# Attention and expert block on one core: the first 28 weight pieces begun in SBUF, their PSUM bank lent to attention

## The chip, the cores and the metric

The kernel runs on one core of one Trainium2 chip. The time is device microseconds (us) of that core, the median of several runs. The core has TensorE (PE: matrix products, written only to PSUM), VectorE (DVE), ScalarE (ACT), GpSimd (POOL) and SyncE (SP, which here only issues transfers). Each takes its instructions from its own queue, in the order in which they were put there. PSUM is a small memory of 8 banks; in this kernel one bank is one tile of 128 x 512 fp32. SBUF is the large on-chip memory.

## What is computed

```
q, k, v: 8 batches x 8 heads x 576 x 64, fp32
scores = q @ k^T / 8, masked by blocks of 64 (block_i >= block_j)
attn   = softmax(scores);  x = attn @ v, heads side by side: 4608 x 512
h = x @ w_in  (512 x 2048);  g = h * sigmoid(1.702 h)
out = g @ w_out (2048 x 512)
```

The weights arrive as 64-bit floats. The kernel reads them as pairs of 32-bit words and makes fp32 from them itself.

## The kernel before

**Attention** goes by 32 pairs of heads, n = 0 to 31, four pairs to a batch. For each pair, `prep` (L292) turns q and k with DVE transposes (L297), `score` (L305) writes q k^T into PSUM banks, `weigh` (L340) takes them out with DVE (L351) and applies exp on ACT (L358), `normalise` (L364) works out the reciprocal on DVE (L368, L371) and scales on POOL (L376). In the first eight pairs `flip` (L401) transposes the weights with TensorE through PSUM banks and ACT copies them out (L411, L424); later pairs use DVE and DMA (`turn`, L382). `av` (L429) multiplies by v, and ACT copies the two banks into `xr` (L450, L451).

**The experts** (`moe`, L509) go by 12 tiles of 384 tokens. A tile's hidden units go in 16 steps `fc`: 12 matmuls into the one bank `h` (tile `hp`), the gate on ACT and DVE (L562, L563), a rounding to a high part on ACT (L571) and the low part on POOL (L82, tile `gl`), and nine matmuls of the step before into `acc0` to `acc2`. Every product is made of three: high x high, low x high, high x low.

**Weight conversion.** The weights are 32 pieces of 128 x 512, in an order of w_in and w_out parts. Piece j goes through a chain: SP loads it (L202); `begin(j)` scales its high words on ACT into a tile `bits[j]` (L219); `merge(j)` shifts that tile in place on DVE (L223), joins the sign on DVE (L229, it reads the loaded words and `bits`), and joins the low word's bits on DVE (L234, words and `bits` in, tile `wm` out); `split_weights(j)` rounds to the high part on ACT (L243) and takes the low part on POOL (L82, tiles `wil` and `wol`). `convert` (L246) runs two steps per piece, first `merge(j)`, then `split_weights(j)`, the load of piece j+2 and `begin(j+1)`. The pace is `WEIGHTS_BY` (L36): 13 pieces by head 8, all 32 by head 14.5; the first token tile asks for its pieces too (L543).

Before the change `bits` is a PSUM tile in bank `w3`, one bank for all pieces. So `begin(j+1)` waits until `merge(j)` has read it out.

**Banks.** `bank()` (L89) hands attention its banks in turn. Until the experts begin (`turns["experts"]`, set by the first `split`, L485, which comes after the A V product of pair 3, asked for by pair 4) it turns over seven: `w0`, `w1`, `w2`, `acc0` to `acc2` and `h`. From then on it has `w0` to `w2`, and from pair 9 on `w3` too.

**Output buffers.** The tag `osb` in SBUF has three buffers of 128 x 512 fp32. They hold the rows of the output on their way out (L527), and, before the first output, part of the loaded words of pieces 28 to 31 (`wst`, L197). Pieces 0 to 27 (`2 * len(places)` is 28) are loaded in pairs into rooms that later hold weights (L192).

**Order of the work.** The order of TensorE's instructions is the program's (`mm`, `tr`, L98 to L102). On ACT, DVE, POOL and SP the instructions are put in order when the kernel is built, by their priority (program order, with some raised) and by when their inputs and buffers are expected to be free. The order inside a pair comes from the strings at L26 to L33, where digits are score chunks, `B`, `C` and `a` are flips, `V` the product with v and `L` the preparation of the next pair; `advance` (L592) fills in expert matmuls after each item.

Of the kernel before, what the change touches and what calls it, by code (L numbers as in the profile page):

```python
# [10 lines left out]
F32 = mybir.dt.float32  # L11
# [29 lines left out]
def attention_moe_kernel(  # L41
# [12 lines left out]
    P = 128  # L54
# [9 lines left out]
    HP = H // 2  # L64
# [3 lines left out]
    d2 = ctx.enter_context(tc.tile_pool(name="d2", bufs=2))  # L68
    ps = ctx.enter_context(tc.tile_pool(name="ps", bufs=1, space=PSUM))

    def f(ap):
        return ap.bitcast(F32)
# [13 lines left out]
    turns = {"n": 0, "bank": 0, "experts": False}  # L86
    conv = {"step": 0, "loaded": 0}

    def bank():  # L89
        tags = ["w0", "w1", "w2"]  # L90
        if not turns["experts"]:
            tags += ["acc0", "acc1", "acc2", "h"]
        elif turns["n"] > 2 * HP:
            tags.append("w3")
        turns["bank"] += 1
        return ps.tile([P, 512], F32, tag=tags[turns["bank"] % len(tags)], name="bank")
# [17 lines left out]
    WC = 512  # L114
# [69 lines left out]
    places = [f"{n}{p}{g}" for n, g in (("wo", 3), ("wo", 2), ("wi", 3), ("wi", 2), ("wo", 3), ("wi", 3), ("wo", 3)) for p in "hl"]  # L184
# [28 lines left out]
    bits, whole = {}, {}  # L213

    def begin(j):

        bits[j] = ps.tile([P, 512], F32, tag="w3", name="wm")
        for w, c in parts[j]:
            nc.scalar.activation(out=bits[j][:, c], in_=f(w[..., 1]), func=AF.Copy, scale=2.0**-112)  # L219

# [25 lines left out]
    def convert(upto):  # L246

        while conv["step"] < int(2 * upto):
            j, odd = divmod(conv["step"], 2)
            if odd:  # L250
                split_weights(j)
                if j + 1 < len(pieces):
                    load_weights(j + 3)
                    begin(j + 1)
            else:
                if j == 0:
                    begin(0)
                merge(j)
            conv["step"] += 1
# [45 lines left out]
    def score(n, banks):  # L305
# [6 lines left out]
        for chunks in banks:  # L312

            part = []
            for lo, hi in ((0, 512),) if width(chunks[0]) <= 512 else ((0, 256), (256, S)):
                ss = [bank() for _ in range(2)]
                c = 0
                for i in chunks:
                    a, z = qrange(i)
                    w = min(hi, width(i)) - lo  # L320
                    for hd in range(2):
                        r = slice(hd * D, hd * D + D)

                        mm(
                            out=ss[hd][:, c : c + w], lhsT=qk[n][r, 0, a : a + P],
                            rhs=qk[n][r, 1, lo : lo + w], start=True, stop=True,
                        )
                        part.append((i, hd, lo, lo + w, ss[hd][0 : z - a, c : c + w]))
                    c += w
            todo.append(sorted(part, key=lambda x: (chunks[::-1].index(x[0]), x[2])))  # L330
# [70 lines left out]
    def flip(n, chunks):  # L401

        for i in chunks:
            todo = [(j, hd) for j in range(i) for hd in range(2)]
            for x in range(0, len(todo), 4):
                part = todo[x : x + 4]
                bk = bank()
                for y, (j, hd) in enumerate(part):
                    tr(out=bk[:, y * P : (y + 1) * P], in_=es[i][:, hd, j * P : (j + 1) * P], identity=ident)
                s0 = SLOT[i] + part[0][0]  # L410
                nc.scalar.copy(  # L411
                    out=pw[:, :, s0 : s0 + len(part) // 2].rearrange("p b s h c -> p (s h) b c"),
                    in_=bk[:, 0 : len(part) * P].rearrange("p (x b c) -> p x b c", b=4, c=32),
                )

        bk = bank()
        todo = [(i, hd) for i in chunks for hd in range(2)]
        for y, (i, hd) in enumerate(todo):
            tr(out=bk[0:BLK, y * P : (y + 1) * P], in_=es[i][:, hd, i * P : width(i)], identity=ident)
        src = bk[0:BLK, 0 : len(todo) * P].rearrange("p (x b c) -> p x b c", b=4, c=32)  # L420
        for part in ([0], [1]) if 0 in chunks else (chunks,):
            i, x, a = part[0], 2 * chunks.index(part[0]), 2 if part[0] else 0
            s0 = 9 + max(i, 1)
            nc.scalar.copy(  # L424
                out=pw[0:BLK, a : a + 2, s0 : s0 + len(part)].rearrange("p b s h c -> p (s h) b c"),
                in_=src[:, x : x + 2 * len(part), a : a + 2],
            )
# [237 lines left out]
```

## Time and profile before

| what | value |
|---|---|
| median of 3 runs | 1122.7 us (1121.84 to 1124.51) |
| the profiled execution, its own time | 1120.49 us |
| its span in the trace | 1118.6 us |
| mean granted TensorE clock | 0.992 |
| TensorE matmul busy, weight loads | 1076.4 us (96%), 908.7 us (81%) |
| DVE, ACT, POOL busy | 583.0, 498.6, 406.7 us |

The trace is one execution. Its rows give the start in us from the span's start, the duration in us, the engine, the line in the kernel, the operation, the tile written and those read, the number of instructions merged in the row, and in brackets the idle time before it with what ended that. "PE bank L102 <- ACT turned L411" reads: TensorE's write of a bank by the helper at L102 waited for ACT's write of `turned` at L411. Where a helper issues all the work (L99, L102, L82), the tile names tell which work it is. Times of single instructions are in us in a timeline and in ns where the text says so.

### The profile page before, as it was taken

The page shows a single profiled execution, that of the slowest core. Times are in us where ns is not written, and L with a number is a line of the kernel's source. Part 1 is how long each engine was busy: PE and PEld are TensorE (multiplying, and loading weights), DVE is VectorE, ACT ScalarE, POOL GpSimd, SP SyncE. Part 2 cuts the span into 40 slices and gives each one's busy share as a digit, 9 for nine tenths or more (in the row PEclk, how much of TensorE's full clock was granted, in tenths as well). Part 3 has the DMA queues.
Part 4 walks back from the last instruction along what each step waited for, and adds up shares of the span by engine and source line. Part 5 has one row for each costly group of instructions (what it writes and reads, how often), then busy time and mean ns, then how long its engine had stood idle before and what let it go on. Part 6 is the DMA issues. An engine that isn't in the chain of part 4 may idle for free. (4 is left out here: it accounts for less than half of the span.)

```text
span 1118.6 us, 19977 instructions
## 1 busy us (share of the span) xinstructions
PE 1076.4 (96%) x6960; PEld 908.7 (81%) x6960; DVE 583.0 (52%) x1856; ACT 498.6 (45%) x1321; POOL 406.7 (36%) x509
## 2 busy tenths in 40 slices
PE   5969998999999999999999999999999999999998
PEld 3757776788888888888888888888888888899997
DVE  6776885545545555654555655645545654211210
ACT  5866776434534433534443543444434444322322
POOL 4665664333333332333333333333333233122222
PEclk9979999999999999999999999999999999999999
DMA  8734532332444432343443333344342332200000
GB/s 171 205 89 153 150 73 62 84 79 57 105 86 86 103 80 64 64 98 78 98 101 74 75 93 65 70 108 85 81 107 63 71 85 58 54 29 1 29 1 29
DMA packets 219365, 91.25 MB, mean 82 GB/s; under 512 B 197760, under 2 KB 197760, under 8 KB 219264
## 3 DMA queue, kind: packets, MB, share of 16 engines
q1 hardware_dynamic: 214528, 89.38, 34.0%
q10 hardware_dynamic: 4736, 0.59, 0.3%
q8 instruction: 55, 0.90, 0.3%
q14 instruction: 46, 0.38, 0.1%
HBM read 45.09 MB, written 9.44 MB: 49 GB/s over the span
## 5 line engine op out<-in xcount | busy, mean ns | idle before, releaser
L82 POOL TENSOR_TENSOR gl<-g,gh 128x384 fp32r<-128x384 f32 x192 | 194.7, 1014 | 551.5 <-ACT gh L571 449.1
L99 PE MATMUL hp<-xh,wih 128*128 128x384 f32 x768 | 264.7, 345 | 7.9 <-DVE g L563 6.9
L563 DVE SCALAR_TENSOR_TENSOR g<-g,hp 128x384 f32<-128x384 f32 x192 | 105.9, 552 | 319.1 <-ACT g L562 317.8
L99 PE MATMUL hp<-xh,wil 128*128 128x384 f32 x768 | 258.4, 336 | 0.1
L562 ACT ACTIVATE g<-hp 128x384 f32<-128x384 f32 x192 | 94.1, 490 | 359.8 <-PE hp L99 354.8
L99 PE MATMUL hp<-xl,wih 128*128 128x384 f32 x768 | 253.9, 338 | 0.4 <-DVE xl L82 0.4
L99 PE MATMUL acc<-woh,gh 128*128 128x512 f32 x576 | 233.9, 406 | 0.0
L99 PE MATMUL acc<-wol,gh 128*128 128x512 f32 x576 | 226.9, 394 | 0.0
L99 PEld LDWEIGHTS hp<-xh,wih 128*128 128x128 f32 x768 | 144.2, 188 | 34.1 <-DVE g L563 23.1
L99 PE MATMUL acc<-woh,gl 128*128 128x512 f32 x576 | 167.9, 393 | 0.3 <-POOL gl L82 0.3
L571 ACT CAST gh<-g 128x384 fp32r<-128x384 f32 x192 | 98.4, 513 | 156.5 <-DVE g L563 156.4
L99 PEld LDWEIGHTS hp<-xh,wil 128*128 128x128 f32 x768 | 144.3, 188 | 6.5 <-POOL wil L82 0.7
L358 ACT ACTIVATE e<-e,mx 64x64 f32<-64x64 f32 (+4 forms) x240 | 132.3, 552 | 37.6 <-DVE mx L351 37.6
L376 POOL TENSOR_TENSOR e<-e,sm 64x64 f32<-64x64 f32 (+1 forms) x192 | 113.6, 612 | 95.0 <-DVE sm L371 46.5
L99 PEld LDWEIGHTS hp<-xl,wih 128*128 128x128 f32 x768 | 143.6, 188 | 1.3 <-DVE xl L82 1.3
L99 PE MATMUL bank<-qk 64*128 64x320 f32 (+4 forms) x768 | 122.5, 428 | 14.5 <-DVE qk L297 11.1
L99 PEld LDWEIGHTS acc<-woh,gh 128*128 128x128 f32 x576 | 107.9, 187 | 34.2 <-issue 10.5
L99 PEld LDWEIGHTS acc<-woh,gl 128*128 128x128 f32 x576 | 107.8, 188 | 25.9 <-POOL gl L82 1.2
L99 PEld LDWEIGHTS acc<-wol,gh 128*128 128x128 f32 x576 | 108.3, 188 | 16.7 <-POOL wol L82 0.3
L351 DVE CUSTOM_DVE_ANT_0 e<-bank,mask 64x64 f32<-64x64 f32 (+4 forms) x240 | 89.7, 417 | 56.9 <-PE bank L99 52.8
L385 DVE STREAM_TRANSPOSE turned<-e 128x384 f32<-128x384 f32 (+1 forms) x192 | 92.3, 499 | 48.8 <-POOL e L376 48.3
L99 PEld LDWEIGHTS bank<-qk 64*128 64x128 f32 x768 | 69.6, 193 | 54.2 <-issue 25.4
(50 smaller groups left out, 956.0 us busy)
## 6 DMA issues: line engine op xcount, KB each, us to landing
turned<-turned SPq DMA_DIRECT2D x192, 80.0 KB, 2.1
turned<-turned SPq DMA_DIRECT2D x96, 112.0 KB, 2.2
raw<-in_q_dram SPq DMA_DIRECT2D x128, 72.0 KB, 2.4
out_dram<-osb SPq DMA_DIRECT2D x36, 256.0 KB, 2.2
raw<-in_k_dram SPq DMA_DIRECT2D x120, 72.0 KB, 2.6
turned<-turned SPq DMA_DIRECT2D x96, 88.0 KB, 2.1
words<-in_moe_w_in_dram SPq DMA_DIRECT2D x16, 512.0 KB, 6.3
vp<-in_v_dram SPq DMA_DIRECT2D x60, 128.0 KB, 2.4
```

Source lines behind the costliest of these rows:

```text
L82: eng.tensor_tensor(out=out, in0=in0, in1=in1, op=ALU.subtract)
L99: return tc.keep_in_program_order(nc.tensor.matmul(**kw))
L351: nc.vector.tensor_tensor_reduce(out=e[0:m, hd, lo:hi], in0=s, in1=mk, op0=ALU.add, op1=ALU.min, scale=-0.125, scalar=3e38 if lo == 0 else ...
L358: nc.scalar.activation(out=e[0:m, hd], in_=e[0:m, hd], func=AF.Exp, scale=-1.0, bias=mx[0:m, i, hd : hd + 1], accum_out=sm[0:m, i, hd : hd ...
L376: nc.gpsimd.tensor_tensor(out=x, in0=x, in1=sc.to_broadcast([m, width(i)]), op=ALU.mult)
L385: nc.vector.transpose(out=tw[:, :, SLOT[i] : SLOT[i] + i, hd].rearrange("p b j c -> p j b c"), in_=e[:, hd, 0 : i * P],)
L562: nc.scalar.activation(out=g, in_=hp[:, 0:tt], func=AF.Tanh, scale=1.702)
L563: nc.vector.scalar_tensor_tensor(out=g, in0=g, scalar=1.0, in1=hp[:, 0:tt], op0=ALU.add, op1=ALU.mult)
L571: nc.scalar.copy(out=gh, in_=g)
```

## The change

`bits[j]` of pieces 0 to 27 becomes an SBUF tile under the tag `osb`, three buffers in turn. Pieces 28 to 31 stay in `w3`. `bank()` includes `w3` as long as fewer than 56 conversion steps (two for each of the 28 pieces) have been made, and, as before, from pair 9 on. So attention turns over eight banks before the experts begin, four from then until the last four pieces, three from there to pair 8, and four after. No instruction is added or taken away.

```
         tags = ["w0", "w1", "w2"]
         if not turns["experts"]:
             tags += ["acc0", "acc1", "acc2", "h"]
-        elif turns["n"] > 2 * HP:
+        if turns["n"] > 2 * HP or conv["step"] < 4 * len(places):
             tags.append("w3")
...
     def begin(j):

-        bits[j] = ps.tile([P, 512], F32, tag="w3", name="wm")
+
+        if j < 2 * len(places):
+            bits[j] = d2.tile([P, WC], F32, tag="osb", name="wb", bufs=3)
+        else:
+            bits[j] = ps.tile([P, WC], F32, tag="w3", name="wb")
         for w, c in parts[j]:
             nc.scalar.activation(out=bits[j][:, c], in_=f(w[..., 1]), func=AF.Copy, scale=2.0**-112)
```

## The prediction

> **What bounds the kernel now.** I read the page first, then the table of windows over the time in which weights are converted, then TensorE's timeline there, then the rows of the conversion's tile `wm`, then DVE, ACT and GpSimd around the stalls.
>
> The page, span and first engine line:
>
> ```profile
> span 1118.6 us, 19977 instructions
> PE 1076.4 (96%) x6960; PEld 908.7 (81%) x6960; DVE 583.0 (52%) x1856; ACT 498.6 (45%) x1321; POOL 406.7 (36%) x509
> ```
>
> TensorE bounds the kernel, and its work isn't touched. What an edit can win is TensorE's idle time, and this edit acts only while pieces 0 to 27 are converted, from the start to about 166 us. Five windows from 28 to 168 us, header and sum (after the time: each engine's busy us):
>
> ```profile
> core 0: us, PE busy (x) PEld busy (x) DVE busy (x) ACT busy (x) POOL busy (x), PEclk, DMA share, GB/s
> sum 140.00, PE 124.80 PEld 98.44 DVE 106.91 ACT 100.16 POOL 88.93; mean PE 24.96 PEld 19.69 DVE 21.38 ACT 20.03 POOL 17.79
> ```
>
> TensorE is idle for 140 - 124.8 = 15.2 us there, DVE is busy for 76% and GpSimd for 64%. TensorE's timeline shows which idle times end with a bank coming free (score or transpose into `bank`) and which with data:
>
> ```profile
> 47.49 1.53 PE L99 MATMUL bank<-qk 64*128 64x320 f32 x6 [0.90 <-DVE mx L351]
> ...
> 58.69 0.76 PE L99 MATMUL bank<-qk 64*128 64x192 f32 x8 [2.52 <-DVE qk L297]
> ...
> 63.16 2.37 PE L102 MATMUL bank<-ident,turned 128*128 128x128 f32 x10 [3.12 <-ACT xr L450]
> 66.33 3.88 PE L99 MATMUL bank<-qk 64*128 64x320 f32 x8 [0.80 <-ACT turned L424]
> ...
> 100.58 0.63 PE L102 MATMUL bank<-ident,turned 128*64 128x128 f32 x4 [1.42 <-ACT turned L411]
> ...
> 129.40 0.63 PE L102 MATMUL bank<-ident,turned 128*64 128x128 f32 x4 [1.60 <-ACT turned L411]
> ...
> 157.62 0.63 PE L102 MATMUL bank<-ident,turned 128*64 128x128 f32 x4 [0.46 <-ACT turned L411]
> ```
>
> L411, L424, L450 and L351 each empty a bank, and none writes what the waiting score or transpose reads: these waits are for a bank. Only the 2.52 us for `qk` is data.
>
> **Part 1: one bank more for attention.** After the experts begin, flips 2 and 3 take four banks out of three: the fourth (the x4 group) waits until the first is copied out. With four banks it takes the bank of a score that DVE had read earlier. So 1.42 + 1.60 + 0.46 = 3.48 us go. What comes next, the matmuls of `hp`, has its inputs long before. In the first four pairs the bank is used again after eight turns and not seven: 0.90 us go at 47.49. At 63.16 the flip of pair 3 takes B1 to B4: B1 was free, B2 is seven turns after the first bank of pair 3's A V product, and so waits for `xr`. With eight, B2 finds a free bank and B3 waits instead: 4 of the 10 transposes, 4/10 x 2.37 = 0.95 us, move into the wait. At 66.33 the first head's bank no longer waits for L424, the second's 4 of 8 matmuls are 1.9 us later: 0.80 us go. Sum of part 1: -6.1 us. It isn't more if ACT keeps its order, since these two ACT copies come late:
>
> ```profile
> 62.44 0.58 ACT L451 COPY xr<-bank 128x512 f32<-128x512 f32 x1
> ...
> 65.87 0.41 ACT L424 COPY turned<-bank 64x128 f32<-64x128 f32 x2
> ```
>
> **Part 2: the conversion's own instructions.** Rows of `wm` (min/median/max in ns), the copy to SBUF at L243, and who waited:
>
> ```profile
> L223 DVE TENSOR_SCALAR wm<-wm x32: 658/699/700, 18.1 to 180.3; 128x512 uint32<-128x512 uint32 x32
> L219 ACT ACTIVATE wm<-words x28: 612/633/662, 13.2 to 159.3; 128x512 f32<-128x512 f32 x28
> L229 DVE SCALAR_TENSOR_TENSOR wm<-words,wm x28: 660/693/697, 18.8 to 160.7; 128x512 uint32<-128x512 uint32 x28
> L234 DVE SCALAR_TENSOR_TENSOR wm<-words,wm x28: 639/682/689, 19.8 to 161.7; 128x512 uint32<-128x512 uint32 x28
> L243 ACT CAST wih<-wm x16: 605/620/631, 20.5 to 162.4; 128x512 fp32r<-128x512 f32 x16
> ...
>   DVE wm L223: 15.9, 18
> ```
>
> L219 into SBUF: the nearest row is L243, of the same size and written to SBUF, 620 ns beside 633, so 28 x 0.013 = 0.4 us less on ACT to, say, as much more; ACT isn't the last to finish at these stalls by that much, and I take nothing. L229 and L234 with both inputs in SBUF: the nearest rows are an expert subtraction with both inputs in SBUF, and a scaling wholly in SBUF for L223:
>
> ```profile
> L82 DVE TENSOR_TENSOR xl<-xr,xh x48: 543/557/1284, 76.2 to 1043.8; 128x384 fp32r<-128x384 f32 x48
> ```
>
> ```profile
> L378 DVE TENSOR_SCALAR e<-e,sm x48: 511/517/521, 212.5 to 951.2; 128x576 f32<-128x576 f32 x48
> ```
>
> 557 ns for 384 elements is no faster per element than 693 for 512, so L229 and L234 cost the same when nothing is in the way. L378 does 576 elements in 517 ns; L223 on 512 should fall from 0.70 to between 0.46 (in proportion) and 0.52: I take 0.48, 28 x 0.22 = -6.2 us of DVE. If uint32 shifts don't have that speed, it is 0.
>
> **Part 3: DVE and GpSimd in each other's way.** That maximum of 1284 ns is the price of part 2. DVE, then GpSimd, at two places:
>
> ```profile
> 56.38 0.91 DVE L368 TENSOR_SCALAR sm<-sm 128x2 f32<-128x2 f32 x1
> ...
> 73.00 0.15 DVE L368 TENSOR_SCALAR sm<-sm 128x2 f32<-128x2 f32 x1
> ...
> 76.24 2.14 DVE L82 TENSOR_TENSOR xl<-xr,xh 128x384 fp32r<-128x384 f32 x2 [0.47 <-PE bank L99]
> ```
>
> ```profile
> 55.45 1.81 POOL L376 TENSOR_TENSOR turned<-turned,sm 128x448 f32<-128x448 f32 x2
> ...
> 76.72 1.25 POOL L376 TENSOR_TENSOR turned<-turned,sm 128x448 f32<-128x448 f32 x1
> ```
>
> The same two-element L368 takes 0.15 us alone and 0.91 when it starts inside GpSimd's work: it ends at 57.29, 0.03 after GpSimd's 57.26. The two subtractions took 2.14 us where two medians are 1.11, and GpSimd's own instruction beside them 1.25, where the pair above gives 0.91. So a DVE instruction wholly in SBUF (L368's kind) or with two SBUF inputs (L82's kind) and a GpSimd instruction go one after the other. Today no conversion row shows it: L223 to L234 have minimum and maximum within 50 ns, though GpSimd is busy for 64% of the time. After the change all three, 84 instructions, are of these kinds.
>
> The Trainium skill, SBUF — State Buffer, section "Who interferes with whom", says this as a rule: an instruction of DVE with two SBUF inputs, or in a mode that uses both its ports, and one of GpSimd exclude each other, the later one blocking until the first is done. It speaks against this change, and the rows above agree with it. By its words a blocked instruction waits for the whole rest; the sum would then have half a GpSimd instruction (0.43 us) a time, 84 x 0.635 x 0.43 = 22.9, and the forecast below would be 1.6 us later.
>
> My own price: the 104 GpSimd instructions of the window average 88.93/104 = 0.86 us; half is 0.43, and 0.12 of the blocked instruction lies within the wait (0.15 - 0.03). So 0.635 x 0.31 = 0.20 us each. From below, all of L368 between 28 and 168 us (busy us, mean ns):
>
> ```profile
> L368 DVE TENSOR_SCALAR sm<-sm 128x2 f32<-128x2 f32 x24 | 7.4, 308 | 4.1 <-ACT turned L358 3.6
> ...
> L368 DVE TENSOR_SCALAR sm<-sm 64x2 f32<-64x2 f32 x6 | 1.8, 306 | 0.4 <-ACT turned L358 0.3
> ```
>
> 9.2 - 30 x 0.15 = 4.7 us of waiting, 0.16 each; from above, the two subtractions, (2.14 - 1.11)/2 = 0.52. I take 0.20, near the lower: 84 x 0.20 = 16.8 us more, less 6.2, so DVE has 10.6 us more in a window with 33.1 us idle.
>
> How much of that reaches TensorE? Behind a blocked L223, L229 or L234 in DVE's queue stand the gate L563, score reads L351 and the transposes L297. Who waited for L368 in the window:
>
> ```profile
>   POOL turned L376: 0.8, 1
>   PEld bank L99: 0.4, 1
> ```
>
> With the 0.76 us at 56.38, which stood ahead of the L297 that ended TensorE's 2.52 us idle time, TensorE felt 0.4 + 0.76 = 1.2 of 4.7 us, a quarter. The gate's slack agrees with less than the whole:
>
> ```profile
> 91.12 0.55 DVE L563 SCALAR_TENSOR_TENSOR g<-g,hp 128x384 f32<-128x384 f32 x1 [0.84 <-ACT g L562]
> ```
>
> ```profile
> 92.83 0.33 PE L99 MATMUL hp<-xh,wih 128*128 128x384 f32 x1
> ```
>
> Here the bank `h` is free at 91.67 and wanted at 92.83: one block of up to 1.16 us is hidden, two in a row aren't. So part 3 costs TensorE 10.6/4 = +2.7 us, between 0 (all in slack) and 10.6.
>
> **Part 4: the buffers `osb` and SP's queue.** Pieces 28 and 29 are loaded into `osb` too. Before, three loads found three buffers; now `bits[27]` holds one, and the load of piece 29 must wait until `merge(28)` is over. In SP's queue it already stands for long, and behind it are the loads of later heads:
>
> ```profile
> 146.71 18.04 SPq L202 DMA_DIRECT2D wst<-in_moe_w_out_dram  x4
> ```
>
> ```profile
> 169.38 0.75 DVE L234 SCALAR_TENSOR_TENSOR wm<-wst,wm 128x256 uint32<-128x256 uint32 x2
> ```
>
> ```profile
> 175.15 1.29 POOL L82 TENSOR_TENSOR wol<-wm,woh 128x512 fp32r<-128x512 f32 x1 [1.52 <-ACT woh L243]
> ```
>
> ```profile
> 180.91 0.39 PE L99 MATMUL acc<-woh,gh 128*128 128x512 f32 x1
> ```
>
> `merge(28)` ends at 170.1, and SP is held till then and not till 164.8. Piece 29 is whole at 176.4 and used at 180.9: a load that begins 5.3 us later meets 4.5 us of cover: between 0 and 0.8 us, and I take 0; without the cover it is 5.3.
>
> **Sum.** -6.1 + 2.7 + 0 = -3.4 us. On the profiled execution, 1120.5 us in all (1118.6 span), that gives 1117.1; the median of the runs is 2.2 us higher than this execution, so 1122.7 - 3.4 = 1119.3. The parts' bounds give 1116.6 (nothing of part 3 is felt) to 1127.2 (all of it).
>
> **Rivals.** First, **DVE fills up** (slower). If every conversion instruction meets GpSimd as the two subtractions did, 0.52 us each, DVE gets 84 x 0.52 - 6.2 = 37.5 us more and has 33.1. The 4.4 us over reach TensorE whole, of the rest a quarter, 8.3: 12.7 - 6.1 = +6.6, 1129.3. Place: 56 to 168 us, at `hp` behind L563 and at scores behind L297. It cancels the gain from 24.4 us net, that is (24.4 + 6.2)/84 = 0.36 us each. For it: once both queues are full they take turns, a whole instruction each. Against: 0.16 on L368. The Trainium skill's section named above is the same mechanism as a rule, and it doesn't say how often the two meet.
>
> Second, **the knot at 56 to 74 us comes loose** (faster). One `w3` forces L219 behind the last merge; DVE waited 15.9 us for it, 18 times. With three buffers L219 can be put earlier, ACT then doesn't hold L451 behind conversions, and the 3.12 us go whole, 2.2 more. With less idle time the clock may hold. Windows of 4 us, and the same groups at full clock:
>
> ```profile
> 64.00:68.00 4.00, 3.20 (x13) 2.20 (x12) 3.24 (x14) 3.22 (x13) 1.28 (x2) 0.50 0.87 225
> ```
>
> ```profile
> 34.52 1.98 PE L99 MATMUL bank<-qk 64*128 64x320 f32 x8
> 36.42 1.31 PE L102 MATMUL bank<-ident,turned 128*128 128x128 f32 x10
> ...
> 70.14 2.39 PE L102 MATMUL bank<-ident,turned 128*128 128x128 f32 x10
> ```
>
> At a granted 0.50 the scores took 3.88 and not 1.98, the transposes 2.37 and 2.39 and not 1.31: 4.0 us. Together -6.2 more: 1113.1. Against it: the 2.52 us for `qk` isn't a bank's, stands ahead of the clock's fall, and hangs on the DVE queue that the change loads more.
>
> Third, **given back**: TensorE meets the next late thing instead (scaled weights from GpSimd, a `qk`), or the order on ACT comes out the same; the gain of part 1 halves to 3 and part 3 takes it: 1122.7.
>
> **How the numbers follow.** Forecast 0.42, DVE fills up 0.26, knot 0.14, given back 0.18. The runs lie 2.7 us apart, so 0.2% (2.2 us) is about what can be told from no change. Faster: 0.36 of the forecast's 0.42, and the knot: 0.50. Same: 0.05 and 0.15 of the third: 0.20. Slower: the first rival, 0.01 and 0.03: 0.30. The range goes from the knot with part 3 unfelt, 1110.4, to the full DVE, 1129.3, rounded to 1110.5 and 1130. The forecast's own is 1116.6 to 1121.9, with from nothing to half of part 3's 10.6 felt.
>
> **What the profile after would show.** Right: no idle time at the x4 transposes after 84 us; L223 at about 480 ns at its least; L223, L229 and L234 spread up to 1.5 us, DVE busy up by some 10 us between 28 and 168. Wrong: L223 to L234 as tight as now (no exclusion, then -6 or better); mean blocks over 0.36 us; TensorE's idle time between 28 and 168 above 15.2 us; or no half clock around 60 to 74.

## The result and the profile after

| kernel | median, us | runs, us | ratio to before, 95% interval |
|---|---|---|---|
| before | 1122.27 | 1120.21 to 1124.51 | |
| changed | 1158.36 | 1155.55 to 1161.04 | 1.0321 (1.0288 to 1.0354) |

The change makes the kernel slower by 3.2%, some 36 us, where 3.4 us less had been forecast; the time lies outside the range. The profiled execution of the changed kernel took 1155.55 us (span 1153.8), 35.1 us more than that of before. Of the runs of the experiments, one of the kernel with bits in SBUF and the order of before took 5908 us; it is left out of that kernel's median and ratio.

In the code of the changed kernel the lines are 4 further down: L223 is `begin` on ACT, L227, L233 and L238 are the three steps of `merge` on DVE, L247 is the rounding on ACT, L355 the score read, L415 and L428 the copies of the flips, L454 and L455 those of A V.

The page of the changed kernel, its span and the engines' busy times:

```profile
span 1153.8 us, 19969 instructions
PE 1094.3 (95%) x6960; PEld 920.8 (80%) x6960; DVE 603.8 (52%) x1856; ACT 500.1 (43%) x1321; POOL 414.6 (36%) x509
```

TensorE does the same instructions in the same order in both kernels. Its busy time grew by 17.9 us (1076.4 to 1094.3) and its idle time, the span less the busy time, by 17.3 (42.2 to 59.5). DVE has 20.8 us more in as many instructions, GpSimd 7.9, ACT 1.5.

The table of windows over the time of the conversion, of before (first) and after; the columns are PE, PEld, DVE, ACT and POOL busy us, then TensorE's granted clock, the share of the DMA engines and GB/s:

```profile
56.00:84.00 28.00, 19.03 (x127) 14.56 (x126) 22.30 (x53) 17.17 (x48) 17.02 (x19) 0.76 0.35 89
...
140.00:168.00 28.00, 27.38 (x192) 21.47 (x191) 22.79 (x60) 20.59 (x54) 19.30 (x21) 1.00 0.31 72
```

```profile
56.00:84.00 28.00, 20.05 (x150) 14.51 (x150) 25.98 (x57) 18.05 (x48) 17.41 (x18) 0.67 0.36 89
...
140.00:168.00 28.00, 26.48 (x150) 21.11 (x152) 19.19 (x50) 14.72 (x40) 14.51 (x18) 0.76 0.25 60
sum 140.00, PE 113.64 PEld 89.01 DVE 105.75 ACT 85.41 POOL 78.80; mean PE 22.73 PEld 17.80 DVE 21.15 ACT 17.08 POOL 15.76
```

TensorE is now idle for 140 - 113.6 = 26.4 us there, and not 15.2. And the clock falls, after 140 us from 1.00 to 0.76 (0.50 in the first 12 us of that window): that is where the longer busy time comes from, the same matmuls at a lower clock. Between 140 and 168 us TensorE is nearly as busy as before, with 150 instructions and not 192. DVE's and ACT's rows look lighter, but each instruction of the program comes later, so a window holds less of it. At the end of the conversion the delay is whole: the last `begin` of a piece in SBUF starts at 195.4 us, in the kernel before at 159.3.

The rows of the tile `wb` in the changed kernel (min/median/max in ns), and below them who waited:

```profile
L227 DVE TENSOR_SCALAR wb<-wb x32: 405/424/1493, 17.1 to 214.6; 128x512 uint32<-128x512 uint32 x32
L223 ACT ACTIVATE wb<-words x28: 644/672/698, 13.0 to 195.4; 128x512 f32<-128x512 f32 x28
L233 DVE SCALAR_TENSOR_TENSOR wb<-words,wb x28: 675/691/1646, 18.2 to 196.5; 128x512 uint32<-128x512 uint32 x28
L238 DVE SCALAR_TENSOR_TENSOR wm<-words,wb x28: 675/1433/2709, 19.7 to 197.3; 128x512 uint32<-128x512 uint32 x28
...
  ACT woh L247: 19.8, 11
  ACT wih L247: 18.5, 15
```

The shift fell to 405 ns at its least, from 699 in the middle. But each of the three DVE steps, which all had a minimum and a maximum within 50 ns, now reaches 1.5 to 2.7 us, and half of the last ones take over 1.4 us. A piece of the changed kernel's timeline shows what they meet; DVE, then GpSimd:

```profile
130.54 0.42 DVE L227 TENSOR_SCALAR wb<-wb 128x512 uint32<-128x512 uint32 x1
130.88 1.78 DVE L238 SCALAR_TENSOR_TENSOR wm<-words,wb 128x512 uint32<-128x512 uint32 x1
132.59 0.68 DVE L233 SCALAR_TENSOR_TENSOR wb<-words,wb 128x512 uint32<-128x512 uint32 x1
...
133.53 1.75 DVE L238 SCALAR_TENSOR_TENSOR wm<-words,wb 128x512 uint32<-128x512 uint32 x1
```

```profile
130.75 1.37 POOL L82 TENSOR_TENSOR wol<-wm,woh 128x512 fp32r<-128x512 f32 x1 [1.61 <-ACT woh L247]
133.39 1.34 POOL L82 TENSOR_TENSOR wil<-wm,wih 128x512 fp32r<-128x512 f32 x1 [1.28 <-ACT wih L247]
```

L238 of one piece starts 0.13 to 0.14 us after GpSimd has begun the low part of the piece before, and ends 0.54 after GpSimd's end (132.66 against 132.12): it has waited out nearly the whole subtraction. Its own result lets ACT round, and ACT lets GpSimd begin the next subtraction, again just ahead of the next L238. So the chain keeps step with itself, 2.6 us a piece. What stands on ACT behind such a rounding is late; ACT, then TensorE, of the changed kernel:

```profile
137.93 0.62 ACT L247 CAST wih<-wm 128x512 fp32r<-128x512 f32 x1 [1.05 <-DVE wm L238]
...
138.87 0.25 ACT L428 COPY turned<-bank 64x128 f32<-64x128 f32 x1
139.02 0.66 ACT L223 ACTIVATE wb<-words 128x512 f32<-128x512 f32 x1
139.58 0.25 ACT L428 COPY turned<-bank 64x128 f32<-64x128 f32 x1
```

```profile
111.26 0.88 PE L102 MATMUL bank<-ident,turned 128*128 128x128 f32 x6 [2.29 <-DVE mx L355]
...
139.88 1.43 PE L99 MATMUL bank<-qk 64*128 64x320 f32 x2 [5.44 <-ACT turned L428]
...
142.69 0.52 PE L99 MATMUL hp<-xh,wih 128*128 128x384 f32 x1
```

The score at 139.88 waits 5.44 us for a bank that the second L428 empties, and the expert matmul after it takes 0.52 us where the same kind took 0.33 at full clock (92.83, above). The idle time at the x4 transposes is gone, as forecast, as long as attention has four banks (behind the last four pieces, where it has three, one of 1.25 us stands at 221.28 us), but waits of another kind and of up to 5.4 us stand elsewhere. The row at 111.26 is such a flip of 14 transposes: its last six wait for the bank of a score that DVE now reads late.

The build lays the order of ACT, DVE, POOL and SP anew for a changed program. Against before, 205 of ACT's 1008 places hold another instruction, 236 of DVE's 1472, 75 of POOL's 506 and 10 of SP's. So two things changed at once: what the instructions do, and their order.

### The profile page after: what moved, and what is told of

Its sections match the earlier page's. It is cut to its first block, busy times and chain, and to the rows that moved or that the text cites. A ratio compares the mean times of both kernels' runs of the same rounds, so it can differ in the third digit from the quotient of the medians.

```text
span 1153.8 us, 19969 instructions
## 1 busy us (share of the span) xinstructions
PE 1094.3 (95%) x6960; PEld 920.8 (80%) x6960; DVE 603.8 (52%) x1856; ACT 500.1 (43%) x1321; POOL 414.6 (36%) x509
## 5 line engine op out<-in xcount | busy, mean ns | idle before, releaser
L99 PE MATMUL bank<-qk 64*128 64x320 f32 (+4 forms) x768 | 127.2, 435 | 27.8 <-DVE qk L301 9.9
L355 DVE CUSTOM_DVE_ANT_0 e<-bank,mask 64x64 f32<-64x64 f32 (+4 forms) x240 | 89.6, 416 | 56.8 <-PE bank L99 52.7
```

The source lines that it names most:

```text
L99: return tc.keep_in_program_order(nc.tensor.matmul(**kw))
L355: nc.vector.tensor_tensor_reduce(out=e[0:m, hd, lo:hi], in0=s, in1=mk, op0=ALU.add, op1=ALU.min, scale=-0.125, scalar=3e38 if lo == 0 else ...
```

## The experiments

The theory: DVE's steps wholly in SBUF, or with two SBUF inputs, and GpSimd's instructions exclude each other, and the time that DVE loses reaches TensorE. The rivals: the turns of the banks do the damage; the three buffers let the chain run too close; the new order does it, whatever lies in SBUF. An "order of before" below means that the order of every instruction on ACT, DVE, POOL and SP is that of the kernel before, held by added order constraints that ask for no waiting (`NoSync`). All times of an experiment stand beside runs of the kernel before on the same chip, whose medians lie between 1122.85 and 1123.51 us.

**Bits in SBUF, banks as before (order by the build).**

```
-        bits[j] = ps.tile([P, 512], F32, tag="w3", name="wm")
+        bits[j] = d2.tile([P, WC], F32, tag="osb", name="wm", bufs=3) if j < 2 * len(places) else ps.tile([P, WC], F32, tag="w3", name="wm")
```

> The changed kernel with attention's banks as before (seven, then three, w3 unused until piece 28); the begun tiles stay in the three SBUF output buffers. Exclusion of DVE and GpSimd: all of the loss is in the SBUF tiles, so 1150 to 1166 us, a few us above the changed kernel if the fourth bank was worth its 3.5 us there too. Order of the build (three buffers let conversions be packed ahead of attention's copies): the same, 1150 to 1166. Banks (the turns over eight and four banks put attention behind the wrong release): the time falls back to 1120 to 1128.

Measured: 1158.73 us, ratio 1.0313 (1.0292 to 1.0334). The loss is whole without a bank turned.

**The same with one SBUF buffer for all pieces**, so that `begin(j+1)` waits for `merge(j)` as it did on `w3` (`one` is a list that starts empty).

```
+        bits[j] = (one or one.append(d2.tile([P, WC], F32, tag="osb", name="wm", bufs=3)) or one)[0] if j < 2 * len(places) else ps.tile([P, WC], F32, tag="w3", name="wm")
```

> The begun tile in SBUF, but one buffer for all of pieces 0 to 27, written again only when the piece before is merged, as the PSUM bank was; banks as before. Exclusion: it is as strong as in the changed kernel, the rows of the two merges reach 1.3 to 2 us, and the time is 1140 us or more. Order of the build: a single buffer keeps the conversion chain as loose as before, so most of the loss goes, 1120 to 1132 us, though merges may still be blocked here and there.

Measured: 1152.98 us, ratio 1.0262 (1.0232 to 1.0291). The three buffers are not the cause; at most 6 us of it.

**Begun in SBUF, shifted into PSUM:** ACT still writes three buffers in SBUF, but the shift writes `w3`, so no step of `merge` has more than one SBUF input, and none lies wholly in SBUF (the code is shortened to what it does for pieces 0 to 27).

```
-        u = bits.pop(j).bitcast(U32)
+        u0, u = bits.pop(j).bitcast(U32), ps.tile([P, WC], F32, tag="w3", name="wm").bitcast(U32)
-            out=u, in0=u, scalar1=3, scalar2=None, op0=ALU.logical_shift_left
+            out=u, in0=u0, scalar1=3, scalar2=None, op0=ALU.logical_shift_left
```

> Begun in three SBUF buffers, but the DVE shift writes into the PSUM bank w3, so that each of the three DVE instructions has one SBUF operand at most; banks as before. Exclusion: no blocking, merges within 0.66 to 0.70 us, shift about 0.7 us, time 1116 to 1126 us. Order of the build: three buffers pack the conversions just the same, so 1135 us or more with tight DVE rows.

Measured: 1127.63 us, ratio 1.0033 (1.0021 to 1.0044). The rows of `wm` in this kernel:

```profile
L223 DVE TENSOR_SCALAR wm<-wm x32: 664/694/699, 17.6 to 188.3; 128x512 uint32<-128x512 uint32 x32
...
L229 DVE SCALAR_TENSOR_TENSOR wm<-words,wm x28: 681/695/697, 18.4 to 169.3; 128x512 uint32<-128x512 uint32 x28
L234 DVE SCALAR_TENSOR_TENSOR wm<-words,wm x28: 671/686/689, 19.3 to 170.0; 128x512 uint32<-128x512 uint32 x28
```

All three are tight again, and 31 of the 35 us that the first experiment lost are gone; what is left puts the time a little above the 1116 to 1126 us expected without blocking. The shift's lower price is gone with them: out of SBUF and into PSUM it takes 0.69 us.

**The turns of the banks alone.** Only the line in `bank()` is changed; pieces and attention then share `w3`.

> The kernel before with the change to the bank turns alone: attention turns over w3 too (eight, then four until piece 28), and the begun tiles stay in w3, so the bank is shared. Exclusion and order: no blocking of merges; the fourth bank's waits of 1.4, 1.6 and 0.5 us at the flips may go, the sharing adds waits of its own: 1118 to 1130 us. Banks: the loss of the changed kernel shows here, 1140 us or more.

Measured: 1160.05 us, ratio 1.031 (1.0286 to 1.0335). DVE's rows are tight here; the waits of TensorE between 28 and 230 us (us, times, longest) are of another kind:

```profile
PE bank L102 <- DVE wm L234: 26.0, 6, 7.0
PE bank L99 <- DVE wm L234: 9.3, 5, 2.9
```

Attention waits for a bank that holds a piece until L234. So this kernel says that the two halves of the change belong together, and nothing on blocking; as a test of the banks it was a poor choice.

**The order held.** The first experiment, the whole change, and the shift into PSUM, each with the order of before:

> Begun in the three SBUF buffers, banks as before, and the order of the instructions in every engine's queue pinned to that of the kernel before, instruction for instruction. What is left of the change is only where the begun tile lies. Exclusion of DVE and GpSimd: 1145 to 1160 us, as with the build's own orders. Order of the build: 1120 to 1128 us, since nothing is packed differently any more, even if some merges are blocked.

> The whole change, SBUF buffers and attention's bank turns, with every queue pinned to the order of the kernel before. Exclusion: as the run with banks before in the same call, less up to 3.5 us if the fourth bank's waits at the flips go. Order of the build: 1117 to 1122 us, better than the kernel before by the bank waits.

> Begun in three SBUF buffers, shifted by DVE into the PSUM bank w3, queues pinned to the order of the kernel before. No DVE instruction has two SBUF operands and none is in the way of GpSimd. Both theories: 1121 to 1126 us, as before; then the 4 us that the same kernel lost with the build's own order were that order. If it is still 1127 or more, writing the begun tile to SBUF costs something by itself.

| order of before | median, us | ratio to before, 95% interval |
|---|---|---|
| bits in SBUF, banks as before (three runs) | 1147.96 | 1.0225 (1.0206 to 1.0243) |
| the whole change | 1140.49 | 1.0165 (1.0136 to 1.0195) |
| shift into PSUM | 1123.97 | 1.0011 (1.0000 to 1.0023) |

The rows of `wm` in the first of these kernels:

```profile
L223 DVE TENSOR_SCALAR wm<-wm x32: 426/888/1541, 18.8 to 208.5; 128x512 uint32<-128x512 uint32 x32
...
L229 DVE SCALAR_TENSOR_TENSOR wm<-words,wm x28: 673/693/2831, 19.6 to 186.7; 128x512 uint32<-128x512 uint32 x28
L234 DVE SCALAR_TENSOR_TENSOR wm<-words,wm x28: 674/692/1565, 20.6 to 189.9; 128x512 uint32<-128x512 uint32 x28
```

With one and the same order, bits in SBUF cost 24.9 us (1147.96 - 1123.09). The turned banks give 7.5 of it back, more than the 3.5 that had been allowed, so the change with the order of before costs 17.4. The other 17.9 us (1158.36 - 1140.49) are the new order. The three steps of the 28 pieces take 25.2, 27.0 and 23.5 us here, and 11.8 (28 x 0.42), 19.3 and 19.0 with nothing in the way: 25.5 us are lost to blocking, 13.4 of them by the shift. In the changed kernel it is the last join that loses most (36.0 us).

**One step alone in SBUF**, the last join, whose input is moved; order of before (the code is again shortened to pieces 0 to 27).

```
+        v = d2.tile([P, WC], F32, tag="osb", name="wm", bufs=3).bitcast(U32)
-                out=u[:, c], in0=w[..., 1], scalar=0x80000000, in1=u[:, c],
+                out=v[:, c], in0=w[..., 1], scalar=0x80000000, in1=u[:, c],
-                out=z[:, c], in0=w[..., 0], scalar=29, in1=u[:, c],
+                out=z[:, c], in0=w[..., 0], scalar=29, in1=v[:, c],
```

> One of the three conversion instructions made to have two SBUF inputs: begun and shifted in the PSUM bank, the sign join writes into an SBUF buffer, and only the last join reads two SBUF operands; 28 instructions can be blocked, not 84; queues pinned to the order of the kernel before. Exclusion: in proportion to the blocks, a third to a half of the loss of the kernel with all three, 1130 to 1142 us; if the loss comes only once DVE is full, under 1127. Order of the build: 1120 to 1127 us.

Measured: 1128.33 us, ratio 1.0043 (1.0026 to 1.006):

```profile
L234 DVE SCALAR_TENSOR_TENSOR wm<-words,wm x28: 637/692/1529, 20.1 to 167.2; 128x512 uint32<-128x512 uint32 x28
```

Of the three steps only the one with two SBUF inputs is spread. DVE's busy time is 5.3 us more (588.3), GpSimd's 5.1 (411.8), and the time 5.2 (1128.33 - 1123.09). A third to a half of the whole loss had been expected, and it is a fifth. The last join took 23.0 us in 28 here, 23.5 in the kernel with all three steps in SBUF and 19.0 before: in this order it has only 4.5 of the 25.5 us that the three steps lose together, and it loses 4.0 here.

**What a us of DVE, and one of GpSimd, is worth,** with no blocking in play. First each sign join is done twice (28 x 0.69 = 19.3 us of DVE more), then a quarter of each low part (some 10 us of GpSimd by the estimate); both with the order of before.

```
-        for w, c in parts[j]:
+        for w, c in parts[j] * (2 if j < 2 * len(places) else 1):
```

> The kernel before, its begun tile in the PSUM bank, with the sign join of pieces 0 to 27 done twice (the second changes nothing), 28 x 0.69 = 19.3 us more of DVE and nothing that GpSimd could block; queues pinned to the order of the kernel before. If DVE's idle time is no slack (each engine's fixed queue waits on the others'), DVE's time reaches TensorE whole or more: 1140 to 1150 us. If the recorded prediction's quarter holds for DVE time as such, 1126 to 1130 us, and then it is the blocking with its second side, GpSimd held up, that cost so much.

```
-        subtract(nc.gpsimd, lo, f(z), f(hi))
+        [subtract(nc.gpsimd, lo[:, x], f(z)[:, x], f(hi)[:, x]) for x in [slice(0, WC)] + [slice(0, 128)] * (j < 2 * len(places))]
```

> The kernel before with a quarter of each weight piece's low part (128 of 512 columns, pieces 0 to 27) taken once more on GpSimd, 28 times about 0.35 us, some 10 us, the time by which GpSimd's own instructions grew in the kernel with SBUF tiles and pinned order; queues pinned to the order of the kernel before. If GpSimd's delay is half of the cost: 1130 to 1136 us. If only DVE's delay counts: 1123 to 1126 us.

Measured: 1141.62 us with the joins doubled, ratio 1.0171 (1.0156 to 1.0186), and 1124.9 with the longer low parts, ratio 1.002 (1.001 to 1.003). So 19.3 us more on DVE cost 18.8 us (1141.62 - 1122.85), all but the whole. In the kernel with the longer low parts GpSimd is busy for 12.5 us more (419.2) and not 10, and that cost 2.05 us, a sixth. The page of the kernel with the joins doubled:

```profile
span 1139.5 us, 20005 instructions
PE 1086.1 (95%) x6960; PEld 914.8 (80%) x6960; DVE 601.3 (53%) x1884; ACT 499.2 (44%) x1321; POOL 407.0 (36%) x509
```

DVE is busy for 53% of that span, and yet it has no slack to give where the joins stand.

**What the banks are worth without blocking.** These kernels leave out the conversion of pieces 0 to 27: in place of shift and joins stand three DVE transposes of about the same length, out of one SBUF tile each, so that the engines are as loaded as before. The order is that of before; the first has the banks of before, the second the changed ones.

```
+        if j < 2 * len(places):
+            parts.pop(j)
+            y, z = (x.bitcast(F32) for x in (bits.pop(j), room("e1" if j % 2 else "wm", [P, WC], U32, "wm")))
+            for x in range(3):
+                nc.vector.transpose(out=(z, y, z)[x], in_=(y, z, y)[x])
+            whole[j] = z.bitcast(U32)
+            return
```

> Leaves out the conversion of pieces 0 to 27: instead of shift and joins DVE makes three 32 x 32 block transposes of the begun tile between SBUF buffers, which have one SBUF operand each, so the weights are not the reference's; banks as before, queues pinned to the order of the kernel before. A control: DVE transposes of 128 x 512 take about 0.69 us as the joins do, and nothing is blocked: 1120 to 1126 us.

> As the control of the same call, with attention's bank turns of the changed kernel: eight, then four banks, since w3 is free until piece 28. What a bank is worth without any blocking. The recorded prediction's part 1: 6 us under the control, 1114 to 1119. If a bank is worth only what the lateness of the other engines makes it worth: within 2 us of the control. If as much as with blocking, 8 us under it.

Measured: 1124.1 us, ratio 1.0019 (1.001 to 1.0029), and 1125.11, ratio 1.0015 (1.0001 to 1.0029). Between these two the bank is worth nothing that can be told. (A kernel of the same kind with the changed banks, in the next experiment, ran at 0.9992, with no partner on the banks of before; so some 3 us can't be excluded, but 6 can.) TensorE's waits between 28 and 168 us show where the gain went; banks of before, then changed:

```profile
PE bank L99 <- DVE qk L304: 3.9, 3, 2.5
PE bank L102 <- ACT turned L418: 3.7, 3, 1.6
PE bank L102 <- ACT xr L457: 3.0, 1, 3.0
```

```profile
PE bank L99 <- DVE qk L304: 5.7, 3, 2.5
PE bank L99 <- ACT turned L418: 1.9, 3, 0.9
...
PE hp L99 <- POOL wil L82: 1.4, 1, 1.4
PE bank L102 <- ACT xr L458: 1.3, 1, 1.3
...
PE bank L102 <- ACT turned L418: 0.5, 1, 0.5
```

The waits of the transposes for L418 (the flips' copy) and for `xr` fell from 6.7 us to 1.8. TensorE then waits for `qk` 1.8 us longer, and 1.4 for the low part `wil` (0.3 before). Of the 4.9 us won, 2.9 are lost again there, and the clock takes more; the same stretch as one window, first with the banks of before:

```profile
28.00:168.00 140.00, 122.98 (x931) 97.21 (x932) 106.96 (x305) 100.42 (x275) 88.31 (x102) 0.95 0.47 129
```

```profile
28.00:168.00 140.00, 125.06 (x900) 98.95 (x897) 106.14 (x304) 99.35 (x273) 87.63 (x101) 0.91 0.47 130
```

TensorE is idle for 2.1 us less, but at a clock of 0.91 and not 0.95, and has got through fewer instructions. That is not one execution alone: over the ten runs of each, the mean granted clock is 0.9895 with the banks of before and 0.9864 with the changed ones.

**The order without blocking.** Is the new order bad by itself, or only where DVE and GpSimd run into each other? The same leaving out (two transposes in place within the begun tile, a third into `wm`), with the changed buffers and banks, in the order of the changed kernel and in that of before:

> The changed kernel in which the shift and the two joins of pieces 0 to 27 are three DVE transposes, two within the begun tile and one from it into wm, so that no conversion instruction of DVE can be blocked by GpSimd; the order of ACT, DVE, POOL and SP is the changed kernel's own. It leaves out the conversion of these pieces. Theory 1 (the order that the build makes for the change costs its 17.9 us only together with blocking, because instructions of DVE and GpSimd run into each other in step there): about 1125 us, within 3 us of the same work in the order of before (1125.1). Theory 2 (the order is bad by itself, since ACT and DVE do things too late in it): 1135 us or more, up to 1143.

> The same kernel as e13 (conversion of pieces 0 to 27 left out in the same way, three DVE transposes in its place), with the order of the kernel before. It is e13's partner: both theories expect 1123 to 1127 us, and the difference e13 - e14 is what the order costs without blocking.

Measured: 1138.46 us, ratio 1.013 (1.0115 to 1.0144), in the new order, and 1122.81, ratio 0.9992 (0.9982 to 1.0002), in the old. With the two kernels of the whole change this makes a square of four (medians, us):

| changed buffers and banks | order of before | order of the changed kernel | order costs |
|---|---|---|---|
| without blocking | 1122.81 | 1138.46 | 15.7 |
| with blocking | 1140.49 | 1158.36 | 17.9 |
| blocking costs | 17.7 | 19.9 | |

The four stand beside kernels of before at 1122.27 to 1123.43 us, so a difference of 1 us in the table isn't to be read, and "blocking costs" is net of what the shift gains.

The two causes all but add up: 17.7 + 15.7 = 33.4 of the 35.6 us between the corners. The theory that the order harms only by making DVE and GpSimd keep step, which the timeline around 130 us had suggested, fell. The place shows why. ACT's timeline, the conversion's roundings around that pair of heads, in the old order and in the new, both without blocking:

```profile
116.61 0.62 ACT L256 CAST woh<-wm 128x512 fp32r<-128x512 f32 x1 [1.22 <-DVE wm L232]
...
120.08 0.62 ACT L256 CAST wih<-wm 128x512 fp32r<-128x512 f32 x1 [1.70 <-DVE wm L232]
...
124.10 0.62 ACT L256 CAST wih<-wm 128x512 fp32r<-128x512 f32 x1 [1.06 <-DVE wm L232]
```

```profile
122.56 0.62 ACT L256 CAST wih<-wm 128x512 fp32r<-128x512 f32 x1 [0.46 <-DVE wm L232]
...
124.34 0.62 ACT L256 CAST wih<-wm 128x512 fp32r<-128x512 f32 x1 [0.31 <-DVE wm L232]
...
127.06 0.25 ACT L437 COPY turned<-bank 64x128 f32<-64x128 f32 x1
...
127.78 0.25 ACT L437 COPY turned<-bank 64x128 f32<-64x128 f32 x1
```

The old order has a piece every 3.5 to 4 us with other work of ACT between them, the new one a piece every 1.8 us, with a `begin` and only a few short instructions between two roundings. DVE's three steps a piece take longer than ACT's two, so ACT waits at each rounding, and the flip's copies behind them (L437) come late: TensorE waited 2.45 us for them at 128.08. Later pieces then come too late. In the changed kernel the last of the 28, ACT, then TensorE, which needs it:

```profile
194.42 1.07 ACT L415 COPY turned<-bank 128x512 f32<-128x512 f32 x2 [0.47 <-PE bank L102]
195.38 0.67 ACT L223 ACTIVATE wb<-words 128x512 f32<-128x512 f32 x1
...
197.99 0.62 ACT L247 CAST wih<-wm 128x512 fp32r<-128x512 f32 x1 [1.07 <-DVE wm L238]
```

```profile
198.66 0.69 PE L99 MATMUL hp<-xh,wih 128*128 128x384 f32 x1 [3.63 <-ACT wih L247]
```

The new order puts its `begin` behind the flip's copies L415; in the trace of before its rounding at 162.41 was over when the same copies began at 163.72. The kernel without blocking waits 4.0 us at the same place.

**Which queue's order.** The whole change, with only DVE's order, then only ACT's, fixed to that of before; the build lays the rest.

> The whole change, with only DVE's order fixed to that of before; the build lays ACT, POOL and SP (they differ from before in 138, 12 and 5 places). If the 17.9 us come from DVE's order (sign joins and shifts put next to low parts): about 1140 to 1145 us. If they come from ACT's order: 1152 to 1158.

> The whole change, with only ACT's order fixed to that of before; the build lays DVE, POOL and SP (they differ from before in 139, 13 and 11 places). If the 17.9 us come from DVE's order: 1150 to 1158 us. If they come from ACT's: 1140 to 1145.

Measured: 1149.54 us, ratio 1.0227 (1.0213 to 1.0241), with DVE's, and 1143.84, ratio 1.0179 (1.0165 to 1.0193), with ACT's. ACT's order alone brings back 14.5 of the 17.9 us, DVE's 8.8; they overlap, since the build lays the free queues to fit the fixed one (with DVE's fixed, 138 of ACT's places differ from before and not 205). The first reading, that DVE's order carries it, missed; with DVE's order fixed the time lies between the two ranges expected.

No version that was run beats the kernel before by more than the 0.2%.

## Why the prediction was wrong

The exclusion that it named is what the runs show, and the signs of parts 2 and 3 held. The gain of part 1 did not come, and the two steps that failed worst are the share of DVE's time that reaches TensorE, and the order, which it costed at nothing.

**Part 1, the bank, -6.1 us: failed.** Without blocking the bank is worth 0 within 0.3%, and 0.5% had been forecast. The waits it named went, as it said; what failed is "what comes next has its inputs long before". TensorE met `qk` and `wil` instead, and a lower clock. This is its third rival, with the gain given back whole and not half. With blocking and the order of before, the turned banks did give 7.5 us, and with the build's orders nothing (1158.73 against 1158.36); where the 7.5 come from was not taken apart. So here a bank was worth most where the rest of the change had already cost more.

**Part 2, the instructions, -6.2 us of DVE: right, and undersized.** At its least the shift took 405 to 426 ns, not 480: 28 x (0.70 - 0.42) = 7.8 us. L219 into SBUF took 672 ns in the middle, where 0.4 us less in all, or as much more, had been allowed: 28 x 0.039 = 1.1 us more on ACT. The kernel with the shift into PSUM has that cost too, 669 ns, and runs at 1.0011, so it reaches TensorE with 0.1% at most.

**Part 3, the exclusion: the mechanism right, the price low, the share wrong.** In the order of before DVE grew by 19.9 us (602.9), with 7.8 saved by the shift: 27.7 us. Of these, 25.5 lie in the 84 instructions themselves, 0.30 each and not 0.20 (0.32 in the changed kernel); the rest is in L368 and the expert subtractions. The measured price lies between the prediction's two rows, 0.16 and 0.52, and the lower one was taken. The Trainium skill, SBUF — State Buffer, section "Who interferes with whom", has the later of the two wait for the whole rest of the other's instruction. The trace agrees but for 0.14 us at 130.88, where L238 began 1.24 us before GpSimd's end and lost 1.78 - 0.68 = 1.10.

The step that failed worst is "TensorE felt a quarter": of 19.3 us put on DVE at the same place, without blocking, it felt 18.8. The quarter came from L368, two elements on sums that TensorE rarely waited for, and from a free time of 1.16 us behind one L563. The conversion's steps are another case: they stand ahead of `qk`, of score reads and of the next rounding, and the chain itself is wanted by TensorE. With 19.9 us at nearly the whole and GpSimd's 10.3 us more (417.0) at a sixth, 19.4 + 1.7 = 21 of the 24.9 us come out; the rest was not taken apart.

The other step that failed is the order of the queues. The prediction kept it ("if ACT keeps its order") or let it change for the better, and gave it no cost; it cost 15.7 us without blocking and 17.9 with it.

**Part 4, the buffers, 0: held.** In the kernel without blocking, with the same three buffers and the order of before, SP was held at these loads until 166.9 us, 2.1 later than before, and the time is 0.9992. In the changed kernel no wait of TensorE ends with a transfer.

**The rivals.** "DVE fills up" had the right place and sign. Its mean of 0.52 us was too high (0.30 to 0.32, below its break-even of 0.36), and yet its 1129.3 was too low, because below a full queue it too took a quarter. A queue need not be full to be late. "The knot comes loose" had the order in mind, and only for the better: L219, set free from the last merge, was indeed laid elsewhere, and the new order as a whole cost 15.7 us without any blocking. The half clock around 60 to 74 us stayed, 0.67 and not 0.76 between 56 and 84 us.

**What was named as a sign.** The x4 transposes (while there were four banks), the spread of the three steps and the shift's fall were as it said; TensorE's idle time between 28 and 168 us (26.4, not under 15.2) was the mark against it. DVE's "some 10 us more" is 20.8 over the whole span; in that window it can't be seen, since the work itself moved out of it.

**What stays open.** Why the build lays that order was not tried; that its own expectation of times lets pieces follow each other too closely, once their buffers are free, is argued from the places above and not shown. With the shift into PSUM its order cost 3.7 us (1127.63 against 1123.97), with bits in SBUF and the old banks 10.8 (1158.73 against 1147.96), with the whole change 17.9, so it is no fixed price of three buffers.

## What to carry to other kernels

Before a tile on the way through VectorE is moved from PSUM to SBUF, list which of its instructions will then lie wholly in SBUF or have two SBUF inputs, and what GpSimd does at that time; a first step that writes PSUM leaves every later step one SBUF input, and that kept the two apart here. An engine that is half busy may have no slack at all where the change acts: put known work there (a step done twice) and measure, before a share is guessed. Where a build orders the queues, a change of buffers is also a change of order; run it with the old order held, and the new order on work that can't collide, and the two prices come apart.

## What the runs showed of the hardware

- Shifting 512 uint32 per partition took 0.41 to 0.43 us from SBUF to SBUF when nothing was in the way, and 0.69 from SBUF to PSUM or within PSUM; only the first was ever blocked by GpSimd.
- A DVE stream transpose of 128 x 512 with input and output in SBUF took 0.66 to 0.71 us, and never longer beside GpSimd's work (84 of them, in the kernel without blocking in the new order).
- GpSimd loses too: the low parts `wil`, 1.26 to 1.29 us in the kernel before, reached 1.75 in the changed one. DVE can lose to several in a row: the longest L238, 2.71 us, met three GpSimd instructions that left no gap between them.
